# Retention and a routed expert layer on one core: loads held to three in flight, GpSimd's work timed to VectorE's reads of PSUM, running counts by products with ones, thinner slices of routing

## The chip, the cores and the metric

The kernel runs on one core of one Trainium2 chip. The metric is the device time of one execution in microseconds (us); lower is better. A core has five engines with queues of their own: TensorE (PE: products, with its weight loads PEld), VectorE (DVE), ScalarE (ACT), GpSimd (POOL) and SyncE (SP, which here only issues DMAs). They run side by side and meet at semaphores. SBUF is the on-chip memory of 128 partitions; PSUM holds the results of products, and GpSimd does not read it in this kernel. 16 DMA engines move data between the chip's large memory and SBUF.

## The reference

8 batches with 8 heads, 576 positions and 64 values a head: a causal, decaying attention without softmax, then a layer of 8 experts in which each token goes to its best expert or is skipped.

```python
scores = scale * np.matmul(q, k.transpose(0, 1, 3, 2))
gamma = 1.0 - 2.0 ** (-5.0 - np.arange(H))
Dmat = np.where(rel >= 0, gamma[:, None, None] ** rel[None, :, :], 0.0)
ret = np.matmul(scores * Dmat[None], v)
x = ret.transpose(0, 2, 1, 3).reshape(B * S, H * D)          # 4608 tokens x 512

do_compute = x @ w_skip > 0                                  # others are passed through
logits = xc @ w_gate;  e_idx = argmax(logits);  gate_w = softmax(logits)[e_idx]
y[mask] = gate_w * (relu(xc[mask] @ w1[e]) @ w2[e])          # for each expert e
out[do_compute] = xc + y
```

## The kernel before, in words

The 4608 tokens are 36 tiles of 128. **The attention stage** takes one tile a step (the loop `for g in range(NT)`, L763). A step issues on TensorE, in an order that is written out by hand (L757): the state product of k and v (`state`, L586), scores times values into `pxt` (`values`, L605, product at L614), the older state times q into the same `pxt` (`carried`, L624, product at L635), the scores of the tile after next (`scores`, L542), the transposes of the tile before (`stage_c`, L658), what stands in the list `pe` (`flush`, L161) and, every fourth step, two products for the logits of four tiles (`logits_a`, `logits_b`).

VectorE masks the scores (`causal`, `sc<-psc`) and multiplies `pxt` by the decays (`decayed`, `xt<-pxt`); both read PSUM. `pxt` and `psc` have one buffer each, so a late VectorE holds up TensorE a step later. ScalarE copies states and finished tiles and writes them out by its own DMA queue. GpSimd multiplies v by the decays in place, one step ahead (`scale`, L581); `state` and `values` need that.

**Loads.** q with k, and v with k, come as 512 KB each on SP's queue: ten at once at the start, then one v after `values` (four buffers) and one q after `carried` (six). SP works its queue in order.

**Routing** is woven into the steps. When the logits of a group of tiles (`GROUPS`, 8, 8, 8, 4, 4, 4) are there, `route` (L167), a Python generator, emits small operations on VectorE: the largest logit, the one-hot choice, running counts of tiles per expert (`cum`, one addition a tile), the gates (`gates`, L242), ranks by products with a triangle and with ones (`ranks`, L205), and one comparison per tile of a rank with all slots (`slot_match`, L274), of which TensorE builds the table of slots (`slot_add`). Each `yield` names a cost in nanoseconds; `spare` (L738) takes operations until the budget of the step (1500, in the last two steps 4500) is used up, or until a `WAIT` for the next `flush`. VectorE's operations keep the order in which they are emitted (`vec`, L152), so routing stands ahead of the step's `decayed`.

After the second group the expert with most tokens is known (`choose_first`); `weights` (L714) counts steps from then (ticks), loads its first five chunks of weights at the ticks in `LOADED`, rounds them to a high part on ScalarE two ticks later, and forms the low part on GpSimd in four quarters three ticks later. After the fourth group 256 of its tokens are gathered (`close_first`, two DMAs that GpSimd issues).

**The expert stage.** Three early blocks (`up_early`) still belong to the hand-written part; `experts` (L930) then goes through 8 experts with 8 chunks each, every product in three parts (high x high, high x low, low x high). `close_last` (L1024) ends the last group's routing there, at the third of its steps. A loop at the end (L1040) takes tokens beyond the planned capacity.

## Time and profile before

| | us |
|---|---|
| median of 3 runs | 429.73 |
| the 3 runs | 428.94, 429.73, 430.58 |
| the profiled execution, its own time | 428.82 |
| its span (first to last instruction) | 427.1 |

| engine | busy us | share of the span | instructions |
|---|---|---|---|
| TensorE products | 396.2 | 93% | 4879 |
| TensorE weight loads | 355.8 | 83% | 4879 |
| VectorE | 271.0 | 63% | 625 |
| ScalarE | 152.0 | 36% | 264 |
| GpSimd | 118.4 | 28% | 142 |

The mean granted clock of TensorE was 0.983. 91.79 MB were moved.

How to read what follows: times are us from the start of the span unless marked ns. A row of the timeline is start, duration, engine, line, operation, what it writes `<-` what it reads, how many instructions are merged in it, and in brackets the idle time before it and what ended that. A row of groups ends with the busy time, the mean of one in ns, and the idle time before. A row of waits gives the time in all, how many times, and the longest. A row of the busy times by stretch has the stretch, its length, then busy time (and instructions) of PE, PEld, DVE, ACT, POOL, then the granted clock, the share of the DMA engines and GB/s. A row of DMA issues ends with the size and the median time from issue to landing. Most VectorE operations are recorded at L153, the line of the helper `vec`; they are told apart by their tiles.

### The profile page before, as it was taken

What the parts mean: (1) busy time and instruction counts of PE and PEld (TensorE: products, weight loads), DVE (VectorE), ACT (ScalarE), POOL (GpSimd) and SP (SyncE); (2) the same over time, 40 slices, a digit from 0 to 9 for tenths busy, and PEclk for the clock granted to TensorE, in tenths of its full rate; (3) what the DMA queues carried; (4) which work ended last, traced back from release to release, by engine and by line L of the source; (5) the groups of instructions that cost most, each with busy time, mean ns of one, the idle gap of its engine ahead of it and who ended that gap; (6) DMA issues with size and microseconds to landing.
All of it is one profiled execution on the core that took longest, in us unless ns stands there. A gap on an engine that the chain in (4) does not pass through costs nothing. (4 is left out here: it accounts for less than half of the span.)

```text
span 427.1 us, 11868 instructions
## 1 busy us (share of the span) xinstructions
PE 396.2 (93%) x4879; PEld 355.8 (83%) x4879; DVE 271.0 (63%) x625; ACT 152.0 (36%) x264; POOL 118.4 (28%) x142
## 2 busy tenths in 40 slices
PE   7989989988869859999999999999999999999990
PEld 3868768767658648888999999999999999999990
DVE  3746795794698987658645655865654755656421
ACT  1222322323322333136443434444444445445210
POOL 7232132232444550150330142033141240400302
PEclk9999999999989998999999999999999999999996
DMA  8998989999998633147663365455465565642101
GB/s 317 406 390 316 387 307 335 393 313 406 344 354 273 230 119 105 66 132 245 207 212 107 140 199 169 148 187 173 156 204 185 156 212 167 208 132 90 53 0 54
DMA packets 28873, 91.79 MB, mean 215 GB/s; under 512 B 4103, under 2 KB 4231, under 8 KB 28816
## 3 DMA queue, kind: packets, MB, share of 16 engines
q1 hardware_dynamic: 19584, 71.31, 47.9%
q0 software_dynamic: 3616, 9.86, 6.7%
q10 hardware_dynamic: 5616, 9.82, 6.1%
q8 instruction: 40, 0.66, 0.6%
q14 instruction: 17, 0.14, 0.1%
HBM read 76.80 MB, written 14.55 MB: 214 GB/s over the span
## 5 line engine op out<-in xcount | busy, mean ns | idle before, releaser
L143 DVE TENSOR_TENSOR wlo_w<-w,whi_w 128x1024 fp32r<-128x1024 f32 x59 | 71.9, 1223 | 62.4 <-ACT whi_w L142 62.4
L142 ACT CAST whi_w<-w 128x1024 fp32r<-128x1024 f32 x59 | 61.6, 1050 | 61.7 <-PE py L452 59.7
L913 POOL DMA_INDIRECT out<-rs,sidx x24 | 32.8, 1367 | 157.7 <-DVE rs L912 154.5
L452 PE MATMUL py<-hhi,whi_w 128*128 128x344 f32 (+6 forms) x224 | 70.7, 316 | 0.0
L452 PE MATMUL ph<-xhi,whi_w 128*128 128x344 f32 (+6 forms) x224 | 68.8, 307 | 0.0
L452 PE MATMUL py<-hlo,whi_w 128*128 128x344 f32 (+6 forms) x224 | 67.8, 303 | 0.0
L452 PE MATMUL ph<-xhi,wlo_w 128*128 128x344 f32 (+6 forms) x224 | 67.8, 302 | 0.0
L452 PE MATMUL py<-hhi,wlo_w 128*128 128x344 f32 (+6 forms) x224 | 67.7, 302 | 0.0
L452 PE MATMUL ph<-xlo,whi_w 128*128 128x344 f32 (+6 forms) x224 | 67.6, 302 | 0.0
L584 POOL TENSOR_TENSOR v<-v,tt_sb 128x512 f32<-128x512 f32 x36 | 37.9, 1054 | 91.6 <-DMA v<-qkv 50.2
L664 ACT COPY xn<-px 128x512 f32<-128x512 f32 x36 | 21.1, 587 | 91.0 <-PE px L662 68.3
L153 DVE TENSOR_TENSOR sc<-psc,mask 128x512 f32<-128x512 f32 x72 | 46.2, 683 | 10.5 <-PE psc L549 5.4
L460 ACT ACTIVATE hhi<-ph 128x344 fp32r<-128x344 f32 (+8 forms) x61 | 26.0, 427 | 64.9 <-PE ph L452 64.9
L614 PE MATMUL pxt<-sc,v 128*64 128x128 f32 x576 | 40.4, 283 | 7.7 <-DVE xt L153 5.6
L153 DVE TENSOR_TENSOR xt<-pxt,gt_sb 128x256 f32<-128x256 f32 x72 | 27.1, 417 | 28.2 <-PE pxt L635 26.1
L452 PEld LDWEIGHTS py<-hhi,whi_w 128*128 128x128 f32 x224 | 42.2, 188 | 0.9
L452 PEld LDWEIGHTS ph<-xhi,whi_w 128*128 128x128 f32 x224 | 42.2, 189 | 0.2
L452 PEld LDWEIGHTS ph<-xlo,whi_w 128*128 128x128 f32 x224 | 42.3, 189 | 0.1
L452 PEld LDWEIGHTS py<-hhi,wlo_w 128*128 128x128 f32 x224 | 42.2, 189 | 0.0
L452 PEld LDWEIGHTS py<-hlo,whi_w 128*128 128x128 f32 x224 | 42.2, 189 | 0.0
L452 PEld LDWEIGHTS ph<-xhi,wlo_w 128*128 128x128 f32 x224 | 42.2, 188 | 0.0
L614 PEld LDWEIGHTS pxt<-sc,v 128*64 128x64 f32 x576 | 32.3, 141 | 10.9 <-DVE xt L153 6.1
(177 smaller groups left out, 608.3 us busy)
## 6 DMA issues: line engine op xcount, KB each, us to landing
w<-w SPq DMA_DIRECT2D x64, 512.0 KB, 3.6
q<-qkv SPq DMA_DIRECT2D x36, 512.0 KB, 7.5
v<-qkv SPq DMA_DIRECT2D x36, 512.0 KB, 6.3
out<-xn ACTq DMA_DIRECT2D x36, 256.0 KB, 5.7
out<-rs,sidx POOLq DMA_INDIRECT x24, 3.9
xg<-out,gidx POOLq DMA_INDIRECT x21, 4.1
gt_sb<-gtab ACTq DMA_DIRECT2D x1, 256.0 KB, 5.6
wg_sb<-wg ACTq DMA_DIRECT2D x1, 64.0 KB, 6.6
```

The source lines that it names most:

```text
L142: nc.scalar.copy(hi, t)
L143: nc.vector.tensor_tensor(lo, t, hi.bitcast(F32), ALU.subtract)
L153: ins = getattr(nc.vector, name)(*args, **kw)
L452: nc.tensor.matmul(ps, x, y, start=first and n == 0, stop=last and n == 3 * len(terms) - 1)
L460: nc.scalar.activation(hi, ph, AF.Relu)
L584: nc.gpsimd.tensor_tensor(v, v, vt_sb[:, place(g), :].unsqueeze(2).broadcast_to([P, H, D]), ALU.mult)
L614: nc.tensor.matmul(pxt[a % 2][halves[j], a // 2, :], v[:, head(a, r), :], sc[:, r, a, :], start=a < 2, stop=t == 0 and a >= NPR - 2, skip_ ...
L664: nc.scalar.copy(xn, px)
L913: put = nc.gpsimd.indirect_dma_start(out=out, out_offset=bass.IndirectOffsetOnAxis(ap=sidx[:n, k, e : e + 1], axis=0), in_=rs[:n], in_offs ...
```

## The change

- Every load of q, v and of the first expert's five chunks waits until the third-last one has landed (`paced`), so that three are under way.
- `scale(g + 1)` moves behind `carried(g)` and waits for the last of its products; the low parts of the weights go into a list of quarters, of which two are taken right after it in each step (`lower`). Both keep their order on GpSimd.
- The running count is kept per group, not per tile: TensorE adds up the tiles inside a group by products of `ones` with each tile's one-hot mask. 8 (or 4) additions and a cast on VectorE become one reduction and one addition; TensorE gets 8 (or 4) products for one. `gates` loses one operation.
- The costs in the yields are raised, so a step's budget takes fewer operations; the budget is 2100 from step 28 on, and 4500 is gone.
- The ticks of the loads are (1, 4, 7, 9, 10) in place of (0, 3, 5, 8, 10).
- At the end, the transposes of the first gathered tokens move ahead of the last logits, and the last group's routing is ended between the early blocks, not in `experts`.

```diff
+FLIGHT = 3
 SPARE = 1500
+LATE = 2100
...
-LOADED = (0, 3, 5, 8, 10)
+LOADED = (1, 4, 7, 9, 10)
...
-    cum = const.tile([P, NT + 1, NE], F32, tag="cum", name="cum")
+    cum = const.tile([P, len(GROUPS) + 1, NE], BF16, tag="cum", name="cum")
...
-        yield 130
+        yield 210
...
-        for t in range(n):
-            vec("tensor_tensor", cum[:, t0 + t + 1, :], cum[:, t0 + t, :], mk[:, t, :], ALU.add)
-            yield 100
-        cb = rt.tile([P, n + 1, NE], BF16, tag="cb", name=f"cb_{t0}")
-        vec("tensor_copy", cb, cum[:, t0 : t0 + n + 1, :])
-        yield 150
...
         def ranks():
             nc.tensor.matmul(pr, utri, mb, start=k == 0, stop=False, skip_group_check=True)
-            nc.tensor.matmul(pr, ones, cb[:, :n, :], start=False, stop=True, skip_group_check=True)
+            for t in range(-1, n - 1):
+                x = cum[:, k, :] if t < 0 else mb[:, t, :]
+                nc.tensor.matmul(
+                    pr[:, (t + 1) * NE :],
+                    ones,
+                    x.unsqueeze(1).broadcast_to([P, n - 1 - t, NE]),
+                    start=False,
+                    stop=t == n - 2,
+                    skip_group_check=True,
+                )
...
+        some = rt.tile([P, NE], F32, tag="some", name=f"some_{t0}")
+        vec("tensor_reduce", some, mk.rearrange("p t e -> p e t"), axis=AX.X, op=ALU.add)
+        yield 220
+        vec("tensor_tensor", cum[:, k + 1, :], cum[:, k, :], some, ALU.add)
+        yield 200
...
-            yield 350
+            yield 300
...
-        vec("tensor_tensor", gt, gt, cp[:, :, 3], ALU.subtract)
-        yield 110
-        vec("tensor_copy", cp[:, :, 4], gt)
-        yield 110
+        vec("tensor_tensor", cp[:, :, 4], gt, cp[:, :, 3], ALU.subtract)
+        yield 200
...
+        def behind(ins, other):
+            tc.add_manual_dep(
+                ins.ins,
+                other.ins.name,
+                mybir.DependencyInfo(mybir.DependencyClass.Sync, mybir.DependencyReason.DATA),
+                reason="paced",
+            )
+
+        def paced(ins):
+
+            if len(flight) >= FLIGHT:
+                behind(ins, flight[-FLIGHT])
+            flight.append(ins)
...
-            nc.sync.dma_start(into[g].rearrange("p s i -> p (s i)"), qkv[g, n])
+            paced(nc.sync.dma_start(into[g].rearrange("p s i -> p (s i)"), qkv[g, n]))
...
-        def scale(g):
+        def scale(g, last=None):
...
+            if last:
+                behind(ins, last)
+            tc.keep_in_program_order(ins)
...
+        def lower(most):
+
+            for _ in range(min(most, len(pieces))):
+                hi, lo, t, m, c = pieces.pop(0)
+                some = lambda x: x[:, m, c : c + NCC // 2]
+                tc.keep_in_program_order(
+                    nc.gpsimd.tensor_tensor(some(lo), some(t), some(hi).bitcast(F32), ALU.subtract)
+                )
...
-            if g + 1 < NT:
-                scale(g + 1)
...
-            carried(g, pxt)
+            last = carried(g, pxt)
+            if g + 1 < NT:
+                scale(g + 1, last)
+            lower(2)
...
-            spare(SPARE if g < NT - 2 else 3 * SPARE)
+            spare(SPARE if g < (KCUT + 4) * NB else LATE)
...
+        lower(len(pieces))
         spare(10 * SPARE)
+        for c, tag in ((0, "sc0"), (2, "sc1")):
+            split(*turn_early(c, tag))
         lt = logits_a(NT // NB - 1)
         flush()
-        for c, tag in ((0, "sc0"), (2, "sc1")):
-            split(*turn_early(c, tag))
...
         up_early(0)
+        flush()
+        up_early(1)
+        spare(10 * SPARE)
+        assert not work
+        for f in range(2, len(EARLY)):
             up_early(f)
...
-    experts({2: close_last, (3, 1): rest})
+    experts({(3, 1): rest})
```

More of the change, by code (lines that the diff above doesn't have):

```diff
@@ L181, in route @@
         vec("scalar_tensor_tensor", oh, ls, 0.0, desc.unsqueeze(1).broadcast_to(nb), ALU.is_equal, ALU.mult)
-        yield 130
+        yield 210
         m2 = rt.tile([P, n], F32, tag="m2", name=f"m2_{t0}")
         vec("tensor_reduce", m2, oh, axis=AX.X, op=ALU.max)
-        yield 130
+        yield 210
         vec("tensor_tensor", oh, oh, m2.unsqueeze(2).broadcast_to(nb), ALU.is_equal)
-        yield 130
+        yield 210
         mk = rt.tile(nb, F32, tag="mk", name=f"mk_{t0}")
@@ L220, in route @@
             vec("tensor_tensor", prb, prv, bump.unsqueeze(1).broadcast_to(nb), ALU.add)
-            yield 130
+            yield 210
             prv = prb
         vec("tensor_tensor", mk, prv, mk, ALU.mult)
-        yield 130
+        yield 210
         vec("tensor_reduce", trank[:, t0 : t0 + n], mk, axis=AX.X, op=ALU.add)
-        yield 130
+        yield 210
         if k == KONE:
@@ L244, in gates @@
         vec("tensor_reduce", sm, ex, axis=AX.X, op=ALU.add)
-        yield 130
+        yield 210
         vec("tensor_scalar", sm, sm, 1e-9, None, ALU.add)
-        yield 110
+        yield 200
         gt = rt.tile([P, n], F32, tag="gt", name=f"gt_{t0}")
         vec("reciprocal", gt, sm)
-        yield 110
+        yield 200
         cp = comps[:, t0 : t0 + n, :]
         vec("tensor_copy", cp[:, :, 2], gt)
-        yield 110
+        yield 200
         vec("tensor_tensor", gt, gt, cp[:, :, 2], ALU.subtract)
-        yield 110
+        yield 200
         vec("tensor_copy", cp[:, :, 3], gt)
-        yield 110
-        vec("tensor_tensor", gt, gt, cp[:, :, 3], ALU.subtract)
-        yield 110
-        vec("tensor_copy", cp[:, :, 4], gt)
-        yield 110
+        yield 200
+        vec("tensor_tensor", cp[:, :, 4], gt, cp[:, :, 3], ALU.subtract)
+        yield 200
         vec(
@@ L305, in choose_first @@
         key = count_key(ps, CNT)
-        yield 130
+        yield 210
         top = rt.tile([P, 1], F32, tag="top", name="top")
         vec("tensor_reduce", top, key, axis=AX.X, op=ALU.max)
-        yield 130
+        yield 210
         vec("tensor_scalar", lead, key, top, None, ALU.is_equal)
-        yield 110
+        yield 200
         ei = rt.tile([P, NE], F32, tag="ei", name="ei")
         vec("tensor_tensor", ei, lead, iota8, ALU.mult)
-        yield 110
+        yield 200
         vec("tensor_reduce", top, ei, axis=AX.X, op=ALU.add)
-        yield 130
+        yield 210
         vec("tensor_copy", lead_id, top)
         regs.append(expert_reg(lead_id[0:1, 0:1]))
-        yield 110
+        yield 200
     def rank_experts(ps):
@@ L361, in close_first @@
             fetch(xg0[:, k, :], gi[:, k : k + 1], nrow)
-        yield 240
+        yield 400
         vec("tensor_scalar", bump, ps[:, c0 : c0 + NE], -1.0, float(CUT), ALU.mult, ALU.add)
         vec("scalar_tensor_tensor", bump, bump, 0.0, lead, ALU.max, ALU.mult)
-        yield 240
+        yield 400
     def fetch(dst, idx, nrow=NTOK):
@@ L492 @@
         q_t, v_t = {}, {}
+        flight = []
+        def behind(ins, other):
[9 more added lines that the diff above has]
+            flight.append(ins)
         def load(into, n, g):
             into[g] = ap.tile([P, 2, DM], F32, tag="qv"[n], name=f"{'qv'[n]}_{g}", bufs=(QBUFS, VBUFS)[n])
-            nc.sync.dma_start(into[g].rearrange("p s i -> p (s i)"), qkv[g, n])
+            paced(nc.sync.dma_start(into[g].rearrange("p s i -> p (s i)"), qkv[g, n]))
         load(q_t, 0, 0)
@@ L579, in decays @@
             )
-        def scale(g):
+        def scale(g, last=None):
             v = v_t[g][:, 0].rearrange("p (h i) -> p h i", h=H)
-            nc.gpsimd.tensor_tensor(v, v, vt_sb[:, place(g), :].unsqueeze(2).broadcast_to([P, H, D]), ALU.mult)
+            ins = nc.gpsimd.tensor_tensor(
+                v, v, vt_sb[:, place(g), :].unsqueeze(2).broadcast_to([P, H, D]), ALU.mult
+            )
+            if last:
+                behind(ins, last)
+            tc.keep_in_program_order(ins)
         def state(g):
@@ L627, in carried @@
             if not t:
-                return
+                return None
             q = q_t[g].rearrange("p s (a i) -> p s a i", a=NPR)
@@ L634, in carried @@
                     j = head(a, r) % 2
-                    nc.tensor.matmul(
+                    last = nc.tensor.matmul(
                         pxt[a % 2][halves[j], a // 2, :n],
@@ L642, in carried @@
                     )
+            return last
         def decayed(g, pxt):
@@ L712 @@
         ticks = []
+        pieces = []
+        def lower(most):
[4 more added lines that the diff above has]
+                    nc.gpsimd.tensor_tensor(some(lo), some(t), some(hi).bitcast(F32), ALU.subtract)
+                )
         def weights():
@@ L719, in weights @@
             ticks.append(None)
-            if n - 3 in LOADED:
-                f = LOADED.index(n - 3)
-                t, (hi, lo) = chunks[f], wq[0, f]
-                for m in range(2):
-                    for c in range(0, NCC, NCC // 2):
-                        some = lambda x: x[:, m, c : c + NCC // 2]
-                        tc.keep_in_program_order(
-                            nc.gpsimd.tensor_tensor(some(lo), some(t), some(hi).bitcast(F32), ALU.subtract)
-                        )
             if n - 2 in LOADED:
                 f = LOADED.index(n - 2)
-                wq[0, f] = parts(chunks[f])
-                tc.keep_in_program_order(nc.scalar.copy(wq[0, f][0], chunks[f]))
+                t = chunks[f]
+                wq[0, f] = parts(t)
+                tc.keep_in_program_order(nc.scalar.copy(wq[0, f][0], t))
+                pieces.extend((*wq[0, f], t, m, c) for m in range(2) for c in range(0, NCC, NCC // 2))
             if n in LOADED:
-                chunks.append(load_w(0, len(chunks), regs))
+                t, ins = load_w(0, len(chunks), regs)
+                paced(ins)
+                chunks.append(t)
         work = []
@@ L795 @@
         g = NT
-        while len(ticks) < LOADED[-1] + 4:
+        while len(ticks) < LOADED[-1] + 3:
             weights()
+        lower(len(pieces))
         spare(10 * SPARE)
+        for c, tag in ((0, "sc0"), (2, "sc1")):
+            split(*turn_early(c, tag))
         lt = logits_a(NT // NB - 1)
         flush()
-        for c, tag in ((0, "sc0"), (2, "sc1")):
-            split(*turn_early(c, tag))
         spare(10 * SPARE)
@@ L810 @@
         up_early(0)
-        assert len(work) == 1 and len(pe) == 1 and len(chunks) == AHEAD
-        for f in range(1, len(EARLY)):
+        assert len(work) == 1 and len(chunks) == AHEAD
+        flush()
[3 more added lines that the diff above has]
+        for f in range(2, len(EARLY)):
             up_early(f)
@@ L827, in count_more @@
         pn = bank("m", "pn")[:, :NE]
-        cb = rt.tile([P, NE], BF16, tag="cbn", name="cbn")
-        nc.vector.tensor_copy(cb, cum[:, NT, :])
-        nc.tensor.matmul(pn, ones, cb, start=True, stop=True)
+        nc.tensor.matmul(pn, ones, cum[:, len(GROUPS), :], start=True, stop=True)
         over = rt.tile([P, NE], F32, tag="over", name="over")
@@ L1022, in experts @@
         assert not between
-    def close_last():
-        flush()
-        spare(10 * SPARE)
-        assert not work
     def rest():
@@ L1048 @@
         reg = expert_reg(mei[0:1, 0:1])
-        ws = [split_w(load_w(0, f, [reg])) for f in range(AHEAD)]
+        ws = [split_w(load_w(0, f, [reg])[0]) for f in range(AHEAD)]
         ps2 = bank("m", "ps2")
```

31 lines of the change are left out of this document (15 added, 16 removed).

## The prediction

> **What bounds the kernel now.** I read the page first, then the busy times by stretch, then the timeline of single steps, then the waits of TensorE.
>
> ```profile
> span 427.1 us, 11868 instructions
> DMA  8998989999998633147663365455465565642101
> ...
> 120.00:130.00 10.00, 6.27 (x113) 5.39 (x106) 9.21 (x25) 1.90 (x3) 5.47 (x8) 0.83 0.85 310
> 240.00:280.00 40.00, 40.00 (x272) 38.85 (x271) 26.54 (x58) 16.88 (x26) 9.73 (x8) 1.00 0.49 164
> ```
>
> The first columns of the last two rows are PE, weight loads, VectorE, ScalarE, GpSimd. From about 165 us on TensorE has no gap: 40.00 of 40 us. The change leaves the work of that stage alone, so the stage can only move as a block: what counts is how much earlier it begins. Before it lies the attention stage of 36 steps, where TensorE has holes (6.27 of 10 us here) while VectorE is nearly full (9.21). The DMA engines are busy too until about 130 us (nines in the slices of 10.7 us), so both have to be asked.
>
> An undisturbed step, and the cycle of steps around it (a step is counted from the first product `pxt<-sc,v` to the next):
>
> ```profile
> 30.20 1.04 PE L614 MATMUL pxt<-sc,v 128*64 128x128 f32 x16
> 40.15 1.09 PE L614 MATMUL pxt<-sc,v 128*64 128x128 f32 x16
> 44.53 1.04 PE L614 MATMUL pxt<-sc,v 128*64 128x128 f32 x16
> ...
> 68.49 1.05 PE L614 MATMUL pxt<-sc,v 128*64 128x128 f32 x16
> 69.47 0.67 PE L635 MATMUL pxt<-q,st 64*64 64x128 f32 x16
> 70.17 0.76 DVE L153 TENSOR_TENSOR xt<-pxt,gt_sb 128x256 f32<-128x256 f32 x2 [1.37 <-PE pxt L635]
> 70.86 1.29 DVE L153 TENSOR_TENSOR sc<-psc,mask 128x512 f32<-128x512 f32 x2
> 70.92 1.04 POOL L584 TENSOR_TENSOR v<-v,tt_sb 128x512 f32<-128x512 f32 x1 [2.14 <-PE psc L549]
> 71.32 0.69 PE L594 MATMUL ps_s<-v 128*64 128x64 f32 x16
> 71.83 1.05 PE L614 MATMUL pxt<-sc,v 128*64 128x128 f32 x16
> ...
> 160.25 1.98 PE L614 MATMUL pxt<-sc,v 128*64 128x128 f32 x16 [2.09 <-issue]
> ```
>
> The plain step is 71.83 - 68.49 = 3.34 us, all of it TensorE's. Steps 5 to 8 are a whole cycle with both logits parts: 44.53 - 30.20 = 14.33, or 3.58 a step. That cycle holds one step without a state product, shorter by some 0.5 us, where the 27 steps from step 8 (40.15) to step 35 (160.25) hold three; so 27 undisturbed steps are 27 x 3.58 + (27/4 - 3) x 0.5 = 98.6 us. They took 120.1. **21.5 us are lost.** Where:
>
> ```profile
> PE pxt L614 <- DVE xt L153: 5.6, 4, 3.1
> PE psc L549 <- issue: 4.1, 3, 1.5
> ...
> 27.73 0.44 PE L549 MATMUL psc<-q 64*64 64x64 f32 x6 [1.47 <-issue]
> ...
> 118.30 1.04 PE L614 MATMUL pxt<-sc,v 128*64 128x128 f32 x16
> 119.49 1.50 DVE L153 TENSOR_TENSOR cum<-cum,mk 128x8 f32<-128x8 f32 x2
> 120.24 2.79 POOL L727 TENSOR_TENSOR wlo_w<-w,whi_w 128x256 fp32r<-128x256 f32 x4
> 123.93 1.36 DVE L153 TENSOR_TENSOR mc<-mks,comps 128x320 bf16<-128x320 bf16 x1
> 125.21 0.74 DVE L153 TENSOR_TENSOR xt<-pxt,gt_sb 128x256 f32<-128x256 f32 x2
> 125.67 0.69 PE L614 MATMUL pxt<-sc,v 128*64 128x128 f32 x4 [3.11 <-DVE xt L153]
> ...
> 153.02 1.05 PE L614 MATMUL pxt<-sc,v 128*64 128x128 f32 x16
> 159.74 0.75 DVE L153 TENSOR_TENSOR xt<-pxt,gt_sb 128x256 f32<-128x256 f32 x2
> ```
>
> Steps 27 (7.37 us) and 34 (7.23) are the worst. In both the eviction of `pxt` comes late, at 125.21 and 159.74, since VectorE is still in the routing that `spare` let it begin; `pxt` has one buffer, so the next step's products wait. In step 27 two additions of eight numbers take 1.50 us beside GpSimd's work, where the group's mean is 0.200 (below), and `mc` takes 1.36. The granted clock fell after that hole: 0.83 over 120 to 130.
>
> **The change part by part.**
>
> ```profile
> L153 DVE TENSOR_TENSOR cum<-cum,mk 128x8 f32<-128x8 f32 x32 | 6.4, 200 | 0.8
> L153 DVE CAST cb<-cum 128x72 bf16<-128x72 f32 (+1 forms) x5 | 1.4, 289 | 0.2
> 134.69 0.46 PE L282 MATMUL ps_m<-mc,r 128*128 128x40 bf16 x12
> ```
>
> *Routing in thinner slices, fewer operations.* The 32 additions and five casts (7.8 us of VectorE) become two operations a group, ten in these five groups, some 2.2 us at 0.2 to 0.25 each; one more operation a group goes in `gates`. The declared costs rise from 130 to 210 and from 110 to 200, so a budget of 1500 buys eight operations in place of twelve, and 2100 buys ten or eleven in place of the 22 that step 34 now holds. A plain step leaves VectorE 3.34 - 0.76 - 1.29 = 1.29 us. Eight operations at about 0.23 are 1.84: 0.55 too many, which hide, as `xt` may be late by 71.83 - 70.93 = 0.90 us before TensorE feels it. A second full step in a row adds up to 1.1 and shows 0.2; steps with eight slot matches show more, steps with logits give back. Going through the yields, routing fills the same steps as before (10 to 13, 18 to 22, 26 to 35), in five runs. Of the 21.5 us, 2.7 are two of the three 'issue' stops; the other 18.8 are this lateness. I leave 1.2 us to each run: 18.8 - 6.0 = **12.8 gained**. The bounds: all of 18.8, or 9.4 less, if a whole scaling of 1.04 us (rows below) comes in between in each of nine full steps, as it did to the additions at 119.49.
>
> *GpSimd timed.* `scale(g+1)` and two quarters of a weight's low part now begin when the last carried product of step g ends, while VectorE reads PSUM. What was hidden comes onto the path here: TensorE's state product of the next step needs `v` scaled.
>
> ```profile
> 25.15 0.46 PE L635 MATMUL pxt<-q,st 64*64 64x64 f32 x16
> 25.78 1.04 POOL L584 TENSOR_TENSOR v<-v,tt_sb 128x512 f32<-128x512 f32 x1 [2.01 <-PE pxt L635]
> L727 POOL TENSOR_TENSOR wlo_w<-w,whi_w 128x256 fp32r<-128x256 f32 x20 | 14.1, 736 | 0.0
> ```
>
> GpSimd started 25.78 - 25.61 = 0.17 us after such a product. With as much again for the way back, the state product can start 0.17 + 1.04 + 0.17 = 1.38 after the carried product; the plain step starts it 71.32 - 70.14 = 1.18 after. That is 0.2 us in each of about 14 plain steps (logits hide it in the others): **2.8 lost**, between none and 8 (0.55 each, if scaling meets a routing operation). Behind the waiting `scale` stand only the quarters and, in step 33, the two gathers. The quarters (2 x 0.74) end 1.15 + 1.5 = 2.7 us after the carried product, before the next scaling.
>
> The Trainium skill ("SBUF — State Buffer", Who interferes with whom) says that a VectorE instruction with two SBUF inputs and a GpSimd one that reads SBUF exclude each other for the whole instruction, and that whichever started first goes on. By it a routing tail that still runs when `scale` starts loses the full scaling each time, and the gain on VectorE's lateness would be 9.4 in place of 12.8; the additions at 119.49 agree with it.
>
> *Loads held to three.* SP's queue gets a wait for the third-last load before each; behind it stand all later loads, and TensorE waits for them.
>
> ```profile
> w<-w SPq DMA_DIRECT2D x64, 512.0 KB, 3.6
> q<-qkv SPq DMA_DIRECT2D x36, 512.0 KB, 7.5
> v<-qkv SPq DMA_DIRECT2D x36, 512.0 KB, 6.3
> ```
>
> Today 2 loads a step of 4.45 us, landing after 6.9 on the mean, are 3.1 in flight, more in the full stretches. With three in flight and a landing time L, the last `v` is the 76th load and lands at about 1 + 25 L. In the new sum it is needed by about 145: L may be 5.75. The w loads (3.6, few in flight) and today's 6.9 bound L; I take the middle, 5.3, as a shorter queue must shorten it: no loss. What it may win are the three stops of TensorE 'for issue' in the midst of its products (4.1 us). The first, at 27.73, falls into a slice with the DMA at nine tenths, in the midst of one run of products; an engine that stops there and waits for no semaphore may lack its instructions, and if these come late behind the loads, fewer loads in flight bring them sooner. I count all **4.1 gained**; bounds 0 and 4.1. The Trainium skill ("Runtime: NRT & Kernel Launch", Instruction fetch mechanics) says that crossing a block of instructions costs one queue bump and is mostly hidden; by it the stops aren't the loads' doing and stay. That is a rival below.
>
> *Counts by products with ones.* 30 more small products (8 for 1 in three groups, 4 for 1 in three): at 0.46 / 12 = 0.04 us, **1.1 lost** on TensorE, between 0 and 3.
>
> *The end.* Step 35 ran at about half speed after the hole of step 34:
>
> ```profile
> 162.16 1.13 PE L635 MATMUL pxt<-q,st 64*64 64x128 f32 x16
> 166.85 0.36 PE L452 MATMUL ph_early<-x,whi_w 128*128 128x256 f32 x1
> 170.22 0.38 ACT L460 ACTIVATE hhi<-ph_early 128x256 fp32r<-128x256 f32 x1 [1.04 <-PE ph_early L452]
> 171.65 0.39 ACT L460 ACTIVATE hhi<-ph_early 128x256 fp32r<-128x256 f32 x1 [1.05 <-PE ph_early L452]
> L368 POOL DMA_INDIRECT xg<-out,gi x2 | 2.8, 1406 | 3.6 <-DVE bump L153 3.3 <-issue 0.3
> ```
>
> 1.98 + 1.13 against 1.05 + 0.67: **1.4 gained** without the hole. Against it, the last group's ranks now stand behind the first early block, 171.65 - 170.22 = 1.4 us of products, and need eight operations of VectorE first (8 x 0.23 = 1.9 us): 0.5 lost. The two gathers (2.8 us) get in line behind two quarters and ahead of the scaling for step 35: with the scaling that is 5.3 us of GpSimd in a step of about 3.8, of which logits leave some 0.5 of slack: 1.0 lost. Together **1.5**, between 0 and 4.
>
> **Sum.** 12.8 + 4.1 + 1.4 - 2.8 - 1.1 - 1.5 = 12.9 us. The profiled execution took 428.82 (span 427.1 and 1.7 around it), the median is 429.73, 0.9 more: 416.8 us.
>
> **The rivals.**
> 1. *The loads are throttled* (slower). If landing takes longer than L = 6.3 us with three in flight, the last `v` lands after 158.3, and step 35 starts, 1.9 us later for scaling and state, no earlier than today's 160.25. Each 0.1 of L is 2.5 us: at L = 6.6 the kernel takes 429.7 + 7.5 = 437. For it: 7.5 and 6.3 today. Against it: today's medians hold the ten loads that are issued at once at the start, and w needs 3.6.
> 2. *The stops stay*: 4.1 less, 421 us. For it: nothing in the page names them. Against it: only three such stops, and the one shown comes with the DMA at nine tenths.
> 3. *The port eats the slices*: `scale` starts just as routing tails run, and nine full steps lose 1.04 each in place of 6.0 together, with scaling late by 0.5: 416.8 + 3.4 + 4.2 = 424. For it: 1.50 for two tiny additions. Against it: the two evictions `sc` take 1.29 at 70.86 beside a whole scaling (70.92), no more than 2 x 0.65.
> 4. *The lateness was cover for something else*, such as the loads at their present pace, which would then end near 429: no change.
>
> **How the numbers follow.** Forecast 0.53 (its own range 411 to 422), rival 1 0.10, rival 2 0.18, rival 3 0.12, rival 4 0.07. A measurement here tells 0.5% (2.1 us) from nothing. Faster 0.53 + 0.18 + 0.12 = 0.83, same 0.07, slower 0.10. The range leaves out rival 1 and half of rival 4, and below it the case that hardly anything of the 18.8 stays: 410 to 428.
>
> **What would show it.** In the new profile: step 27 and step 34 under 5 us; no granted clock below 1.00 between 120 and 165; the 32 additions gone; no 'issue' stop of 1.5 us at L549; state products waiting some 0.2 us for `v`; the first early block near 154 in place of 166.85, and everything after it the same length. The prediction is wrong if SP's loads wait on loads and GpSimd or TensorE on `v<-qkv` for many us, or if the first early block starts as late as now.

## The result, and the profile after

| | median us | lowest to highest | runs |
|---|---|---|---|
| before | 429.99 | 428.94 to 430.58 | 4 |
| after | 448.72 | 445.68 to 449.70 | 4 |

The changed kernel is slower: the ratio is 1.0426, with a 95% interval of 1.0371 to 1.0482. The prediction said 416.8 us and gave "slower" one chance in ten. Its first rival, "the loads are throttled", is what took place.

Two rows of the page of the kernel after:

```profile
span 443.9 us, 11899 instructions
DMA  8899979979777988313865355356465466542101
```

and busy times by stretch, first of the kernel before from the start of its step 8 to that of its step 34, then of the kernel after for the same steps, for 20 us of them and for a part of the expert stage (columns as before: the stretch, its length, PE, weight loads, VectorE, ScalarE, GpSimd, granted clock, share of the DMA engines, GB/s):

```profile
40.15:153.02 112.87, 101.97 (x2284) 83.55 (x2284) 88.98 (x257) 34.69 (x67) 40.71 (x44) 0.98 0.90 327
```
```profile
40.36:167.54 127.18, 107.20 (x2307) 88.19 (x2308) 81.23 (x229) 31.88 (x65) 38.28 (x41) 0.93 0.84 287
66.00:86.00 20.00, 19.96 (x467) 16.54 (x465) 11.91 (x29) 5.57 (x11) 5.67 (x6) 1.00 0.98 330
240.00:280.00 40.00, 40.00 (x263) 38.96 (x262) 22.42 (x31) 17.75 (x28) 8.47 (x6) 1.00 0.48 159
```

Compare the first two rows. VectorE is busy for 81.23 us where it was busy for 88.98: that part of the forecast came true. The steps take 14.3 us longer all the same, so something else holds TensorE now. The DMA engines are not full (a share of 0.84 after 0.90). In the DMA row, where hardly anything but nines and eights stood up to about 130 us, sevens stand among them from 55 us on, and the high digits go on to 175 us. The DMA engines have less to do at a time and take longer over it.

Steps of the changed kernel, by its timeline:

```profile
50.60 0.35 SPq L519 DMA_DIRECT2D v<-qkv  x1
...
52.25 1.07 PE L642 MATMUL pxt<-sc,v 128*64 128x128 f32 x16
...
58.45 1.04 POOL L607 TENSOR_TENSOR v<-v,tt_sb 128x512 f32<-128x512 f32 x1 [7.21 <-DMA v<-qkv]
...
59.54 1.12 PE L622 MATMUL ps_s<-v 128*64 128x64 f32 x16 [4.37 <-POOL v L607]
...
60.45 1.92 PE L642 MATMUL pxt<-sc,v 128*64 128x128 f32 x16
...
128.18 1.05 PE L642 MATMUL pxt<-sc,v 128*64 128x128 f32 x16
132.34 1.21 PE L642 MATMUL pxt<-sc,v 128*64 128x128 f32 x16
140.63 1.92 PE L642 MATMUL pxt<-sc,v 128*64 128x128 f32 x16
...
170.70 1.04 POOL L607 TENSOR_TENSOR v<-v,tt_sb 128x512 f32<-128x512 f32 x1 [2.36 <-DMA v<-qkv]
171.80 1.09 PE L642 MATMUL pxt<-sc,v 128*64 128x128 f32 x16 [1.92 <-DVE sm L156]
...
181.06 0.49 PE L460 MATMUL ph_early<-x,whi_w 128*128 128x256 f32 x2
```

Step 27 (128.18 to 132.34) now takes 4.16 us where it took 7.37. But step 11 (52.25 to 60.45) takes 8.20 and step 28 (132.34 to 140.63) 8.29, where they took 5.22 and 6.29 before. The chain of step 11 can be followed in the rows: SP issues the load of the next tile's `v` at 50.60, GpSimd has stood idle for 7.21 us when it can scale it at 58.45, and TensorE has stood idle for 4.37 us when the state product starts at 59.54. The products that follow take 1.92 in place of 1.07. The first early block begins at 181.06, 14.2 us later than before.

The waits of the whole program, and the DMA issues with their sizes and median landing times:

```profile
SPq L519 <- DMA v<-qkv: 73.7, 31, 7.3
SPq L519 <- DMA q<-qkv: 27.4, 18, 2.6
SPq L135 <- DMA q<-qkv: 14.3, 3, 6.0
POOL v L607 <- DMA v<-qkv: 48.0, 13, 7.2
PE ps_s L622 <- POOL v L607: 12.0, 7, 4.4
PE psc L572 <- issue: 1.1, 2, 0.9
```
```profile
q<-qkv SPq DMA_DIRECT2D x36, 512.0 KB, 6.1
v<-qkv SPq DMA_DIRECT2D x36, 512.0 KB, 5.9
```

SP's queue used to wait for TensorE to give buffers free; now it waits for loads, 101 us for q and v, and more for the first expert's chunks (L135). A load does land sooner than before (6.1 and 5.9 for 7.5 and 6.3), as the prediction expected. It doesn't help, as fewer loads are in flight: the rate is what is in flight divided by the landing time, and it went down.

Where the 16.8 us of the two spans (443.9 - 427.1) lie is told by four marks: the first `pxt<-sc,v` product of steps 8 and 34, the 200th product of the expert stage (its early blocks counted), and its last one. In the table and in the sections behind it each row is one profiled execution; single executions of one kernel differ by several us (the kernel before took 428.13 to 434.54 in 13 runs on one chip), so that differences of a few us between rows decide nothing by themselves.

| kernel | steps 8 to 34 | step 34 to product 200 | product 200 to the last |
|---|---|---|---|
| before | 112.9 | 50.2 | 211.4 |
| after | 127.2 | 52.6 | 211.4 |

14.3 us were lost in the steps and 2.4 at the end of the attention stage. From product 200 on both kernels take 211.4: that stage is moved as a block, as the prediction took it.

### The profile page after: what moved, and what is told of

Same layout as the page of the kernel before. It is cut to its first block, busy times and chain, and to the rows that moved or that the text cites. A ratio compares the mean times of both kernels' runs of the same rounds, so it can differ in the third digit from the quotient of the medians.

```text
span 443.9 us, 11899 instructions
## 1 busy us (share of the span) xinstructions
PE 400.8 (90%) x4909; PEld 359.7 (81%) x4909; DVE 263.1 (59%) x588; ACT 151.1 (34%) x264; POOL 119.0 (27%) x142
## 5 line engine op out<-in xcount | busy, mean ns | idle before, releaser
L156 DVE TENSOR_TENSOR xt<-pxt,gt_sb 128x256 f32<-128x256 f32 x72 | 27.1, 418 | 41.9 <-PE pxt L663 40.2
L642 PE MATMUL pxt<-sc,v 128*64 128x128 f32 x576 | 41.5, 289 | 2.0 <-DVE sm L156 1.9
L460 PEld LDWEIGHTS ph<-xhi,whi_w 128*128 128x128 f32 x224 | 42.2, 189 | 0.2
L460 PEld LDWEIGHTS ph<-xlo,whi_w 128*128 128x128 f32 x224 | 42.2, 188 | 0.1
L460 PEld LDWEIGHTS py<-hlo,whi_w 128*128 128x128 f32 x224 | 42.2, 189 | 0.0
L460 PEld LDWEIGHTS ph<-xhi,wlo_w 128*128 128x128 f32 x224 | 42.2, 189 | 0.0
L460 PEld LDWEIGHTS py<-hhi,wlo_w 128*128 128x128 f32 x224 | 42.2, 188 | 0.0
L622 PEld LDWEIGHTS ps_s<-v 128*64 128x64 f32 x512 | 18.6, 144 | 25.1 <-POOL v L607 17.6
```

Source lines behind the costliest of these rows:

```text
L156: ins = getattr(nc.vector, name)(*args, **kw)
L460: nc.tensor.matmul(ps, x, y, start=first and n == 0, stop=last and n == 3 * len(terms) - 1)
L622: nc.tensor.matmul(ps_s[halves[r], a, :], k[:, head(a, r), :], v[:, head(a, r), :], start=t in (0, NPD // 2) and a == 0, stop=a == NPR - 1 ...
L642: nc.tensor.matmul(pxt[a % 2][halves[j], a // 2, :], v[:, head(a, r), :], sc[:, r, a, :], start=a < 2, stop=t == 0 and a >= NPR - 2, skip_ ...
```

## The experiments

Theory A: three loads in flight throttle the loads. Theory B: GpSimd's timed work does it, since TensorE's state products now wait for a scaling that begins late. The medians, with the kernel before on the same chip (430.8 to 432.3 in these runs):

| run | what differs | median us | ratio to before, 95% interval |
|---|---|---|---|
| x1 | after, no limit on loads | 428.74 | 0.9892 [0.9799, 0.9985] |
| x2 | after, five in flight | 428.58 | 0.9911 [0.9864, 0.9958] |
| x3 | before, three in flight | 449.40 | 1.0386 [1.0302, 1.0469] |
| x4 | after, scaling not timed | 448.87 | 1.0393 [1.0306, 1.0481] |
| x5 | x1, scaling not timed | 428.53 | 0.9877 [0.9821, 0.9934] |
| x6 | x1, end as before | 428.36 | 0.9911 [0.9880, 0.9943] |
| x7 | x6, budgets as before | 429.50 | 0.9929 [0.9888, 0.9970] |
| x8 | before, routing's edits only | 428.41 | 0.9925 [0.9894, 0.9955] |
| x9 | after, four in flight | 430.41 | 0.9977 [0.9935, 1.0019] |
| x11 | x6, routing of step 35 late | 427.46 | 0.9891 [0.9829, 0.9953] |
| x12 | x11, scaling not timed | 429.51 | 0.9960 [0.9924, 0.9996] |
| x13 | x11, an early block first | 427.31 | 0.9885 [0.9834, 0.9937] |
| x14 | x13, five in flight | 426.65 | 0.9889 [0.9852, 0.9926] |

### The limit on loads: x1, x2, x9, x3

The edit of x1; x2 has 5 and x9 has 4 in its place:

```diff
-FLIGHT = 3
+FLIGHT = 1000
```

> The changed kernel with the wait between loads gone (1000 in flight in place of 3); all else stays. Theory A (with three loads under way the DMA engines run dry while one of them finishes the oldest load, so every step waits for its v): 415 to 423 us, as all other edits keep their gain. Theory B (the scaling of v behind the carried products and its fixed order on GpSimd hold up TensorE): still 440 us or more.

> The changed kernel with five loads in flight in place of three. Theory A: between the changed kernel and the unpaced one, near the unpaced one, 418 to 428 us, since a fast DMA engine then has two more loads to go on with. Theory B: 445 to 450 us, as the changed kernel.

> The changed kernel with four loads in flight in place of three. The three in flight took 5.9 to 6.1 us to land and gave 2 loads a step too late; five in flight cost nothing (428.6 us). If what counts is the bytes in flight over one landing time, four carry a third more: 77 loads at 6 us take 116 us in place of 154, which is below the 145 by which they are needed, and the time is that of five in flight, 428 to 431. If each load's last packets leave the engines idle whatever is behind it, four are still short in the stretches where weights and outputs come in between: 434 to 440.

For x3 the kernel before got the limit of three, for q, v and the first expert's chunks, and nothing else:

> The kernel before with nothing changed but that loads of q, v and the first five chunks of weights wait for the third-last one. Theory A: slower than before by 8 to 20 us, 438 to 450. Theory B: 428 to 432, no change.

Three in flight cost 20 us in the changed kernel (448.7 with them, 428.7 without) and 17 in the kernel before (449.4 with them, 432.3 without, on the same chip). Four cost at most a few us (its interval against before is 0.9935 to 1.0019, where that of five is 0.9864 to 0.9958), and five cost nothing that can be measured. In x3 SP waits in the same way, though nothing else was changed:

```profile
SPq L513 <- DMA v<-qkv: 74.5, 32, 7.6
SPq L513 <- DMA q<-qkv: 31.0, 22, 2.6
```

Theory A is shown: the limit alone makes the loss, and taking it out takes the loss out. What is left of the forecast without the limit is a gain of some 3 us in place of 9 (13 less the 4.1 of the stops, which is taken up below).

### GpSimd's timing: x4

The scaling goes back to the head of the step, with no wait and no fixed place on GpSimd:

```diff
-            if last:
-                behind(ins, last)
-            tc.keep_in_program_order(ins)
...
         for g in range(NT):
+            if g + 1 < NT:
+                scale(g + 1)
...
-            if g + 1 < NT:
-                scale(g + 1, last)
```

> The changed kernel with the scaling of v back in its old place, without the wait for the carried products and without a fixed order; loads stay at three in flight. Theory A: 440 to 450 us. Theory B: 422 to 432 us.

448.87 us with the limit of three: theory B falls.

### What three in flight are worth by themselves: x10

A program that only loads, in phases, with a landing time of its own for each (`threew` and `fivew` have writes of 256 KB beside every second load).

> Loads of 512 KB alone, of the same rows of q, k and v, in phases of 24 (6 and 12 for the first two): one, two, three, four, five and ten in flight, then three, five and ten with a write of 256 KB to the output on ScalarE's queue beside every second load. Nothing is computed and the output is zeros. If three in flight are too few by themselves: landing time 5 us or more with three alone, and less than 320 GB/s, rising to 380 to 410 with five and ten. If it is the other traffic of the kernel that makes three too few: three alone land in about 3.9 us at 400 GB/s, as five do in 6.5, and only beside the writes three fall to 250 to 300 GB/s of loads.

The rows of its DMA issues (median landing time last), then the busy times of the middle of these six phases in the same order (the share of the DMA engines and GB/s are the last two columns):

```profile
three<-qkv SPq DMA_DIRECT2D x24, 512.0 KB, 4.7
four<-qkv SPq DMA_DIRECT2D x24, 512.0 KB, 5.1
five<-qkv SPq DMA_DIRECT2D x24, 512.0 KB, 6.4
ten<-qkv SPq DMA_DIRECT2D x24, 512.0 KB, 10.2
threew<-qkv SPq DMA_DIRECT2D x24, 512.0 KB, 5.3
fivew<-qkv SPq DMA_DIRECT2D x24, 512.0 KB, 6.8
```
```profile
65.00:100.00 35.00, 0.00 (x0) 0.00 (x0) 1.00 0.93 331
105.00:135.00 30.00, 0.00 (x0) 0.00 (x0) 1.00 1.01 384
140.00:168.00 28.00, 0.00 (x0) 0.00 (x0) 1.00 1.02 407
175.00:202.00 27.00, 0.00 (x0) 0.00 (x0) 1.00 1.00 399
208.00:247.00 39.00, 0.00 (x0) 0.00 (x0) 1.00 0.97 361
252.00:286.00 34.00, 0.00 (x0) 0.00 (x0) 1.00 1.03 407
```

Three in flight land in 4.7 us with nothing beside them, neither the 5 nor the 3.9 of the two expectations, and give 331 GB/s where five give 407 and ten no more. From five on a load only stands in line longer (6.4, then 10.2) at about the same rate: a long landing time, such as the 7.5 and 6.3 of the kernel before, need not mean slow loads. Beside the writes three give 361 GB/s, of which a fifth is the writes: 289 of loads. An attention step needs two loads, 1.049 MB; at the cycle's 3.58 us a step that is 293 GB/s, at the 4.18 us a step of x1 (108.6 us for 26 steps, below) 251, and the first expert's chunks come on top. So three that are really in flight are about enough in a program that does nothing else, with nothing to spare.

In the kernel there are not three all the time. The trace has the landing signals of every load. From them, on the mean: the loads in flight from 20 to 140 us, the landing time of all loads up to the last `v`, and when that `v` landed, in one profiled execution each.

| kernel | loads in flight | landing time, us | last `v` landed, us |
|---|---|---|---|
| after | 2.6 | 5.59 | 170.5 |
| x3 before, three in flight | 2.6 | 5.70 | 172.1 |
| x9 after, four in flight | 3.1 | 6.25 | 158.1 |
| x2 after, five in flight | 3.3 | 6.5 | 150.1 |
| x1 after, no limit | 3.6 | 6.79 | 141.0 |
| before | 3.6 | 6.85 | 144.9 |

(The 6.1 and 5.9 of the page rest on the 28 loads of q and v for which it has a landing; over all 72 the medians are 5.7 and 5.6.) In the changed kernel three are in flight for 0.66 of that time, two for 0.27, one for 0.08. The reason can be read in SP's rows:

```profile
45.46 4.96 SPq L519 DMA_DIRECT2D q<-qkv  x2
50.60 0.35 SPq L519 DMA_DIRECT2D v<-qkv  x1
58.35 0.33 SPq L519 DMA_DIRECT2D q<-qkv  x1
58.85 0.80 SPq L519 DMA_DIRECT2D v<-qkv  x2
```

`paced` counts loads in the order in which the program makes them, and SP's queue holds them in another order. The q issued at 58.35 is, in the program, the third load after the v issued at 50.60, and waits for its landing at 58.29; in the queue it stands right behind it. The v at 58.85 has to wait only for a q that landed at 52.20, but it stands behind that other q. Of the 74 loads that wait, 18 wait for the last or the last but one ahead of them in the queue, all five of the expert's chunks among them. Where the two orders agree, three do suffice: all loads from 66.0 to 85.5 us wait for the third-last in the queue, 2.9 are in flight and land in 5.8 on the mean, TensorE is busy for 19.96 of the 20 us from 66 to 86, with the DMA engines at 0.98, and steps 14 to 18 take 18.1 us where x1's take 17.9. From 46 to 66 us and from 86 to 140, where they differ, only 2.3 are in flight. No run keeps the queue in the program's order to the end. The nearest is x9, where a limit of four holds 3.1: its median, 430.41, can't be told from before's (the execution in the table was its slowest, 435.77).

Step 11 shows what a single late load costs. This is the changed kernel during its wait:

```profile
54.50:56.50 2.00, 0.68 (x10) 0.42 (x4) 1.97 (x6) 0.00 (x0) 0.00 (x0) 1.00 0.83 306
56.50:58.30 1.80, 0.00 (x0) 0.00 (x0) 0.99 (x4) 0.38 (x1) 0.00 (x0) 0.73 0.21 77
58.50:62.00 3.50, 2.46 (x32) 2.43 (x32) 0.00 (x0) 0.38 (x2) 0.99 (x1) 0.50 0.73 231
```

From 56.50 to 58.30 TensorE does nothing, waiting for `v`, and the DMA engines are busy for 0.21 of the time: a few of them finish the load, and the others have nothing queued, as the next load in SP's queue waits for this one. Of the 16 landing signals of this `v` the first comes at 54.87, the eighth at 55.19, the fourteenth at 56.14 and the last at 58.29. The Trainium skill ("DMA: Bandwidth & Descriptors", Why a DMA increments its semaphore by 16 and not by 1) says that the engines of one transfer finish independently and that only the full count means that all of it has landed; the share of 0.21 ahead of the landing and the spread of the 16 signals agree. After the hole the granted clock is 0.50 for the next stretch, so that a late load is paid for twice.

### Where the rest of the gain went: x5, x8, x6, x7

x5 is x1 with the edit of x4. x8 is the kernel before with the routing's edits alone.

> The changed kernel with no limit on loads in flight and the scaling of v put back ahead of the step, with no wait and no fixed place on GpSimd (only the quarters of the low parts stay pinned). Without a limit and with the scaling timed the kernel took 428.7 us and step 35 began 8.0 us earlier than in the kernel before. If the timing of the scaling earns its part of those 8 us (VectorE's operations are disturbed less), this run loses 2 to 4 us of it: 431 to 433, step 35 at 154 to 156. If the timing is worth nothing and the thinner slices and fewer operations do it all: 428 to 429, step 35 at 151.5 to 152.5, and plain steps 3.34 long again in place of 3.40 to 3.45.

> The kernel before with the routing's edits alone (running counts by products with ones, fewer operations a yield, 2100 from step 28): no limit on loads, the scaling and the weights' halves and the end as before. If routing earns the whole gain on VectorE's lateness: step 35 begins 7 to 9 us earlier than in the kernel before (160.25) and the time is 421 to 424. If the timing on GpSimd is needed for it: 2 to 4 us earlier, 426 to 428.

For x6 the end is put back (x7 has the old budgets as well, 1500, and 4500 in the last two steps):

```diff
-        for c, tag in ((0, "sc0"), (2, "sc1")):
-            split(*turn_early(c, tag))
         lt = logits_a(NT // NB - 1)
         flush()
+        for c, tag in ((0, "sc0"), (2, "sc1")):
+            split(*turn_early(c, tag))
...
-        flush()
-        up_early(1)
-        spare(10 * SPARE)
-    experts({(3, 1): rest})
+    experts({2: close_last, (3, 1): rest})
```

> The changed kernel with no limit on loads in flight and the end of the attention stage ordered as before: the last group's logits ahead of the turning of the first expert's blocks, the five early blocks in one run, the last group's routing closed in the expert stage. Theory 'the new end gives the gain back': of the 8.0 us by which step 35 began earlier without the limit, only 4.8 were left at the first early block and about 1 after the first hundred products of the expert stage; with the old end the first early block should come at about 159.5 to 160.5 and the time at 422 to 424. Rival 'the expert stage loses them for another reason' (what the earlier start runs into: weight loads, instruction packets): 428 to 429 as without the limit, with the loss at the same products.

> As the run with no limit and the old end, and the budgets of steps 28 to 35 as before too (1500, and 4500 in the last two). If the flat budget of 2100 is what keeps step 34 short (7.23 us before, a hole of 3 us), step 34 is over 6 us again here and the time 2 to 4 us above the run with the old end alone: 425 to 428. If the pile left to step 35 and after it by the flat budget is what delays the end, this run is 1 to 2 us below it.

All five, x1 among them, come out at 428.4 to 429.5, with intervals that overlap: each expectation by which one of the edits earns the rest of the gain is missed. The edits to the routing alone (x8) give what the whole change gives without the limit, about 3 us. The marks suggest why the others add nothing:

| kernel | steps 8 to 34 | step 34 to product 200 |
|---|---|---|
| before | 112.9 | 50.2 |
| x8 routing only | 110.6 | 49.6 |
| x5 no limit, scaling not timed | 107.4 | 51.8 |
| x1 no limit | 108.6 | 54.3 |
| x6 no limit, old end | 108.5 | 51.8 |
| x7 no limit, old end and budgets | 103.4 | 53.0 |

These are single executions (x7's, 423.76 us, is one of the two fastest of its twelve), and the time up to step 8 differs too: 40.2 us in before and x1, 41.6 to 42.2 in the others. With that said, what is won in the steps mostly comes back behind step 34. Its hole (7.23 us before) was VectorE doing routing that has to be done before the expert stage can go on; the flat budget leaves the same operations to step 35 and the end. This is step 35 of x1:

```profile
150.97 0.78 DVE L156 TENSOR_TENSOR cum<-cum,some 128x8 bf16<-128x8 bf16 x1
151.67 0.17 DVE L156 TENSOR_REDUCE sm<-ex 128x4 f32<-128x32 f32 x1
151.69 5.13 POOL L751 TENSOR_TENSOR wlo_w<-w,whi_w 128x256 fp32r<-128x256 f32 x6
...
152.43 0.70 DVE L156 TENSOR_SCALAR sm<-sm 128x4 f32<-128x4 f32 x1
153.16 0.18 DVE L156 RECIPROCAL gt<-sm 128x4 f32<-128x4 f32 x1
...
157.88 0.75 DVE L156 TENSOR_TENSOR xt<-pxt,gt_sb 128x256 f32<-128x256 f32 x2
158.35 1.69 PE L699 MATMUL pl<-xt,wg_sb 128*32 128x512 f32 x8 [2.85 <-DVE xt L156]
```

Six quarters run in a row on GpSimd, and beside them and the scaling ahead of them additions of four or eight numbers take 0.70 to 0.78 us, while the reduction and the reciprocal take 0.17 and 0.18. The eviction `xt`, which stands behind all this on VectorE, comes at 157.88, and TensorE has waited 2.85 us for it. The Trainium skill ("SBUF — State Buffer", Who interferes with whom) says that `tensor_scalar` and `tensor_tensor` with two SBUF inputs can be shut out by GpSimd and that `tensor_reduce` never is; the rows agree.

### The end, two more ways: x11, x12, x13, x14

x11 against x6 (x12 has the edit of x4 as well):

```diff
-            spare(SPARE if g < (KCUT + 4) * NB else LATE)
+            spare(SPARE if g < (KCUT + 4) * NB else LATE if g < NT - 1 else 0)
...
-        spare(10 * SPARE)
         lt = logits_a(NT // NB - 1)
-        flush()
         for c, tag in ((0, "sc0"), (2, "sc1")):
             split(*turn_early(c, tag))
         spare(10 * SPARE)
+        flush()
+        spare(10 * SPARE)
         stage_c(NT - 1)
```

x13 against x11 (x14 has `FLIGHT = 5` as well):

```diff
         spare(10 * SPARE)
+        up_early(0)
         flush()
...
-        up_early(0)
```

> No limit on loads, the end as before, and no routing of the last group but one ahead of step 35's eviction: it comes behind the last logits and the turning of the early blocks. In the runs without the limit step 35's eviction waited 3.7 to 4.0 us, for small operations of VectorE that took 0.64 to 0.78 each beside six quarters on GpSimd. If that is what gives back the lead at the end, the first early block comes 6.6 us after step 35's first product in place of 9.7 to 11.5, near 159 to 161, and the time is 424 to 426. If the operations only move, and what follows waits for them, the time stays 428 to 429.

> The same with the scaling of v not timed, as before. If the timing of the scaling is worth something once the end no longer hides it, this run is 2 us or more slower than the one with the scaling timed; if not, they agree within 1 us.

> As the run with the late routing of step 35 and no limit, and the first of the three early blocks (4.3 us of products) ahead of the slot products that waited 3.9 us for VectorE there. If TensorE only stood in line, the wait of 3.9 us is filled: the two hundredth product of the expert stage comes 3 to 4 us earlier than the 201.7 of that run, and the time is 423.5 to 425. If VectorE is the bound to the end, the later early blocks or the ranks wait as much longer, and the time stays 427 to 428.

> The same with five loads in flight. If five are enough also for a shorter attention stage (needed: 2 loads of 512 KB and a write of 256 KB each 3.6 us; five gave 321 GB/s of loads beside writes by themselves, 291 are needed), it agrees with the run without the limit within 1 us. If they are not, 2 to 3 us more.

In x11 the eviction comes at once, but TensorE then waits 3.9 us for the slot matches of the last group but one, where x1 waited 2.85 for the eviction. These waits, for x11, then x13:

```profile
PE ps_m L290 <- DVE r L156: 3.9, 1, 3.9
```
```profile
PE ps_m L290 <- DVE r L156: 1.6, 1, 1.6
```

So the operations only moved, and the time, 427.46, lies between the two expectations, nearer to the second. In x13 an early block of 128x256 products fills part of the wait (3.9 to 1.6), and step 34 to product 200 takes 50.7 where x11 takes 51.6. The mark itself comes 3.8 us earlier in the profiled execution (197.95 after 201.72), as expected, but 2.9 of that lie before step 34, and the expected 3 us don't show in the median (427.31). x12 against x11 is not told apart (intervals 0.9924 to 0.9996 and 0.9829 to 0.9953). x14, with five in flight, agrees with x13 within the 1 us expected, and is a version a little faster than both kernels: 0.9889 of before, 0.9852 to 0.9926.

### What GpSimd costs in the steps: x15, x16

x15 is x13 without `lower(2)` in the steps; x16 leaves out the scaling too. Each was run once, and only steps 8 to 34 are read.

> As the run with the early block first and no limit, with all twenty quarters of the weights' low parts on GpSimd behind the last step in place of two a step. The end gets longer by what GpSimd then still has to do (some 17 us), so only steps 8 to 34 are read. If the quarters beside VectorE's slot matches are what keeps the full steps long, the step from 28 to 29 (6.9 to 7.8 us) falls by 0.5 to 1 us, five slot matches take 2.2 or less in place of 2.9, and steps 8 to 34 take 104 to 105.5. If VectorE's own work keeps them long, they take 107 to 108 as before.

> The same without the scaling of v: that part of the computation is left out, and GpSimd does nothing in the steps. It gives the whole price of GpSimd's work in steps 8 to 34, the wait of the state products for the scaling included (0.06 to 0.1 us a plain step). By the port's account small operations are never long: the excess of VectorE's operations over their shortest falls from 7 to 9 us to under 2, and steps 8 to 34 take 100 to 103. If VectorE's own work is the bound, 105 or more.

Steps 8 to 34 take 109.1 in x15, above both of its expectations, and 104.2 in x16, between the two. The slot matches `r` show best what GpSimd does to VectorE; their shortest, median and longest in ns, in the kernel before and in x16:

```profile
L153 DVE TENSOR_SCALAR r<-iota,trank x28: 302/315/1114, 58.3 to 146.4; 128x384 bf16<-128x384 f16 x28
```
```profile
L156 DVE TENSOR_SCALAR r<-iota,trank x28: 307/314/322, 57.4 to 138.9; 128x384 bf16<-128x384 f16 x28
```

With GpSimd idle no slot match takes over 322 ns; before, six of the 28 take over 600, up to 1114. The excess of VectorE's operations over the shortest of their form, summed over steps 8 to 34, is 9.7 us before, 5.2 with the routing's edits alone (x8), 5.6 in x1, 6.0 in x13, 4.9 in x15 and 1.0 in x16. So GpSimd's work does lengthen VectorE's operations, and the scaling does the larger part of what is left (4.9 to 1.0, after 6.0 to 4.9 for the quarters). The routing's edits alone took away what the whole change takes (1.4 us of it in the additions to `cum`); the timing on GpSimd shows no steady effect (5.6 with it in x1 and 7.8 without in x5, 6.2 with it in the changed kernel and 4.6 without in x4). What all of it is worth in time is not settled: 104.2 against 107.0 in x13 and 109.1 in x15 are single executions, and x7, with GpSimd's work in place and fewer routing operations in steps 28 to 33, takes 103.4.

## Why the prediction was wrong, point by point

**The loads, "no loss": the step that failed.** The prediction put the last `v` at about 1 + 25 L, needed L of 5.75 or less, and took 5.3, the middle between 6.9 and the 3.6 of the weights, "as a shorter queue must shorten it". L came out close: 5.59 on the mean over all loads of the changed kernel, longer than 5.3 and below the 5.75 that was allowed. What failed is the other half of the step, that three loads are always in flight, by which L gives 1 + 25 L. With 5.59 that would be 141, and the last `v` landed at 170.5, since 2.6 were in flight and not three: the wait for the third-last load in the program's order drained SP's queue, which has another order (2.9 in flight from 66 to 86 us, where the orders agree, 2.3 from 46 to 66 and from 86 to 140). So 1 + 25 L holds only with 6.8 in the place of L, the time in which three loads got through, of which 5.59 is landing. In x9, with 3.1 in flight, it holds as it stands: 1 + 25 x 6.25 = 157, and 158.1 in the trace.

That 5.3 came so near was partly luck. The middle of 3.6 and 6.9 had no ground: the 3.6 of the weights is the landing time of loads with few others beside them, and the 6.9 was taken with 3.6 in flight on the mean. Where three did stay in flight (66 to 86 us) a load took 5.8, which would put the last `v` at about 146, an estimate just past the 145 by which it was needed; x10 has 4.7 alone and 5.3 beside writes, where 1.573 MB were needed in about 5.4 (at 293 GB/s). Rival 1, "the loads are throttled", had the outcome, its point of decision (6.3) and its slope of 2.5 us for each 0.1; with 6.8 it gives 442, and the profile took 445.68. Its condition, a landing time over 6.3, was not met. Its chance of 0.10 was too low for a term whose two bounds gave opposite signs.

**VectorE's lateness, 12.8 gained.** The direction was right and the size too large: steps 8 to 34 shrink by 2 to 6 us without the limit (112.9 to 110.6 with the routing's edits alone, to 108.6 in x1, to 107.0 in x13). The 18.8 came from subtracting an undisturbed cycle, and that cycle holds no routing at all: even with GpSimd idle these steps take 104.2, against 94.8 by the prediction's own 3.58 a step. Some of what was called lateness must be TensorE's products for the routing, the stops, and VectorE's own work; no run splits it. And most of step 34's share wasn't lost: it was work done there and not later.

**The 'issue' stops, 4.1 gained.** The effect came in part, and only with the limit that costs 20 us: 4.1 us at the scores before (three stops), 1.1 after, though 2.2 us of a new stop stand at a state product there. Without the limit they stay (the first row is x1's), and with five in flight too (the second is x2's), which is rival 2:

```profile
PE psc L572 <- issue: 4.6, 5, 1.4
```
```profile
PE psc L572 <- issue: 5.8, 5, 1.9
```

In x3 the scores have none, but the state products have 7.6 us put down to 'issue', more than the 4.1. So the loads as their cause are not shown, and what TensorE lacks there is left open.

**The end, 1.4 gained and 1.5 lost.** Step 35's products did get back to 1.16 us in x1. The loss was mis-sized: step 34 to product 200 takes 54.3 in x1 for 50.2, after a step 34 that is 3.8 shorter, so that 7.9 us are lost behind it. The order of the new end and the flat budget both seem to be part of it: from step 35 on the same stretch takes 50.8 in x1, 48.4 with the old end (x6), 43.9 with the old budgets as well (x7) and 43.0 before, in single executions.

**The scaling, 2.8 lost.** Too much: in x1 a plain step takes 3.40 to 3.45 where it took 3.34, so 0.06 to 0.11 in place of 0.2, and the medians of x1 and x5 are equal. Rival 3, the port, shows where the six quarters run in step 35, and not as the 7.6 us over the steps that it was priced at. **The 30 products, 1.1 lost:** nothing of them can be seen in a median.

Of the signs named, step 27 and step 34 did fall under 5 us (4.16 and 4.25 in the changed kernel) and the additions went, while the time rose. The signs that spoke for the loss were those named as such: SP's loads waiting on loads, GpSimd on `v<-qkv`, a late first early block.

## What to carry to other kernels

A limit on loads in flight is a rate limit: bytes in flight over the landing time that holds under this traffic, to be set against what a step consumes. Count what is in flight in the order of the queue that issues the loads, in the trace: a wait for the third-last load of the program, put into a queue with another order, held 2.6 here, and 2.3 in the stretches where it hurt. Nor can a long landing time be turned into a gain by queueing less, where it is time spent in line (x10: 6.4 and 10.2 us at about the same rate). And a hole that an engine's small work makes is only worth what isn't needed soon after: look for who consumes that work before counting the hole as lost.

## What the hardware showed that was not expected

- 512 KB loads alone ran at 331, 384, 407 and 399 GB/s with three, four, five and ten in flight. The last fifth of the rate costs two more in flight and 1.7 us of landing time.
- A wait of 4.37 us of TensorE was followed by a stretch at a granted clock of 0.50 (the third of the rows of step 11), in which the same 16 products took 1.92 us in place of 1.07.
- From the last product of the expert stage to the end of the span lie 12.5 us in the profiles of seven kernels (before, after, x3, x6, x7, x8, x11) and 14.0 to 14.6 in others (x1, x2, x4, x5, x12, x13, x14), with no edit there. No run explains it; it is as large as most of the effects sought here.
